# Leaky slope in PSUM instead of weight-product passes, for the second part of batch 0's MLP blocks

## The chip, the cores and the metric

The kernel runs on one core of one Trainium2 chip. The metric is device time in microseconds (us), the median of the runs.

## The reference

The program is a long convolution by FFT, gated, followed by a two-layer MLP with a leaky ReLU. Cut to what matters:

```python
def _attn_ref(x, v, pos_emb, w1, w2):                 # x, v: (2, 12480, 128)
    h_filt = (np.maximum(pos_emb @ w1, 0.0) @ w2) * window
    u = x * v
    y = irfft(rfft(u, 2*S) * rfft(h_filt, 2*S))[:, :S]   # per batch and channel
    return x * y

def _moe_ref(x, w_in, w_out):                         # 24960 tokens, 128 -> 2048 -> 128
    h = x @ w_in
    g = np.maximum(0.01 * h, h)
    return g @ w_out
```

## The kernel before, in words

The convolution is done as a two-level transform. After an opening stage that transforms batch 0, the MLP starts and runs over `NTL` = 50 blocks of tokens, `widths` columns each: block 0 has 390, the others 512 except block 24 (314) and blocks 48 and 49 (352). Blocks 0 to 24 are batch 0, blocks 25 to 49 batch 1. Each block is worked in `NF` = 16 steps, one for each 128 rows of the hidden layer. Step number `i = k * NF + f` is the clock of everything else: the main loop at the end of `tile_conv_mlp` calls, for each step, `m1(k, f)`, then `m2` of the step `DEEP` = 3 earlier, then the work that `steps` has put down for that step (loads, the inverse transforms `front` of later tokens, the sums `join`), then parts of `finish` for the block before, and lastly pieces of `conv`, the generator that carries batch 1's forward and inverse transforms. All pieces of `conv` are spread evenly over the steps before `SLOTS` (375, that is block 23, step 7). Instructions of an engine run in the order in which this loop issues them.

`m1` makes one tile `mh` of the hidden layer: three TensorE passes of 512 columns (the product is split in high and low parts, `w_in_h` times `zh` and `zl`, `w_in_l` times `zh`) into a PSUM bank, then the non-linearity, and from it the two parts `rh` and `rl`, which `m2` multiplies by `w_out_h` and `w_out_l` in three further passes into the accumulator bank `acc0` or `acc1` (`acc{k % 2}`). There are three ways to the non-linearity:

- `sums(k)`: ScalarE takes the plain ReLU from PSUM as `rh`, VectorE takes max(h, 0) - rh as `rl`; the missing slope, 0.01 times h, comes from three more passes of the block's input `zh`, `zl` by the product of the two weight matrices (`wc_h`, `wc_l`), which `m2` issues at its step 0.
- `wide`: ScalarE writes the leaky ReLU (`Lrelu`, slope 0.01) back into the same PSUM bank; `rh` is copied from there by VectorE where f is odd and by ScalarE where f is even; VectorE takes `rl` from the bank as the difference.
- else (the blocks `OWN`, 2 to 4): the leaky ReLU goes to a buffer in SBUF, and the two parts are taken from there.

`sums(k)` holds for blocks 0, 1 and 5 to 23. In batch 0, tokens that don't go by `sums` are first multiplied by 1/0.99 in `product_of` (`nc.scalar.mul` on `zf`), since the output weights are held times 0.99.

PSUM has eight banks: `mh` three, `cv` two (for `conv`, until it has ended; then for every fourth and fifth `mh` tile of the wide blocks), `io` one, `acc0` and `acc1`. In block k the bank `acc{(k + 1) % 2}` holds the sums of block k - 1 until `finish` has copied them (step 2), and the next block's from step 3 of that block on; `last_transform` uses it for the second of a pair of inverse transforms (`second`; the first of the pair is in `leads`; both are worked at step `turn_at`).

A tile of the `mh` ring can be written again once `rl` of the tile that had the bank is made; and `m2` of step i - 3, right behind `m1` of step i on TensorE, reads that same `rh` and `rl`.

Of the kernel before, what the change touches and what calls it, by code (L numbers as in the profile page):

```python
# [8 lines left out]
F32 = mybir.dt.float32  # L9
# [15 lines left out]
WIDE = 512  # L25
# [5 lines left out]
def tile_conv_mlp(ctx, tc, x, v, pos_emb, w1, w2, w_in, w_out, cf, cr, cg, cb, ci, cw, out):  # L31
    nc = tc.nc
    B, S, D = x.shape
    FO = pos_emb.shape[1]
    DFF = w_in.shape[1]
    NF = DFF // 128
# [72 lines left out]
    def mixed(t):  # L109

        return t.rearrange("p (h i) -> p i h", h=2)

    def plain(t):

        return t.rearrange("p (i h) -> p h i", h=2)

    def split2(t):

        return t.rearrange("p (h i) -> p h i", h=2)
# [44 lines left out]
    def back(dp, parts, c):  # L164

        for s in range(2):
            for j, w in halves(c):
                m = mixed if even(w) else lambda t: t
                three(dp[s][:, w], (mi_h[j][:, s], mi_l[j][:, s]), (m(parts[0][:, s, w]), m(parts[1][:, s, w])))

    def turned(pool, psum, m2, m1):

        ph = pool.tile([128, 2, KH + 1], F32, tag="ph0", name="ph0", bufs=1)
# [62 lines left out]
    with tc.manual_schedule():  # L236
# [228 lines left out]
        def conv1b():  # L465
# [46 lines left out]
            for c in range(NCH + 1):  # L512
# [5 lines left out]
                if c < NCH:  # L518
                    n = chunk(c)[1]
                    w = n * D  # L520
                    h, (th, tl) = hd.pop(c), parts.pop(c)
                    yield
                    up = psc["next"]()
                    for s in range(2):
                        three(up[s][:, :w], (mb_h[:, s], mb_l[:, s]),
                              [i[:, :n, s, :].rearrange("p (h k) d -> p k d h", h=2) for i in (th, tl)])
                    yield

                    us, p1 = sc.tile([128, 2048], F32, tag="s4", name="usp").rearrange(
                        "a (i s w) -> i a s w", i=2, s=2)  # L530
                    ph = pool.tile([128, 2, 512], F32R, tag="ph", name="ph", bufs=1)
                    pl = pool.tile([128, 2, 512], F32R, tag="pl", name="pl", bufs=1)
                    pins[c] = ph, pl
                    for s in range(2):
                        nc.scalar.mul(split2(us[L, s, :w]), plain(up[s][H, :w]), -1.0)
                        o = 1 - s
                        nc.vector.tensor_tensor(out=split2(p1[:, o, :w]), in0=plain(up[o][:, :w]),
                                                in1=split2(h[:, 0, o, :w]), op=ALU.mult)
                        if s:
                            sums(us, p1, h, 0, w)  # L540
                        yield
                        nc.scalar.copy(split2(us[H, s, :w]), plain(up[s][L, :w]))
                        yield
                    sums(us, p1, h, 1, w)
# [41 lines left out]
        ld, cin, z, acc = {}, {}, {}, {}  # L586
# [103 lines left out]
        with ExitStack() as st:  # L690
# [73 lines left out]
            def two(tag):  # L764
                return [psb.tile([128, 512], F32, tag=tag, name=tag + "p", bufs=2) for _ in range(2)]
# [41 lines left out]
            for i, c in enumerate(ORD):  # L807
# [17 lines left out]
                t, es = bins.pop(c), eh.pop(c)  # L825
                hp = two("h")
# [47 lines left out]
        ps = ctx.enter_context(tc.tile_pool(name="ps", bufs=1, space=bass.MemoryType.PSUM, reuse_waits="tile"))  # L874
# [11 lines left out]
        at0 = [sum(widths[:i]) for i in range(len(widths) + 1)]  # L886
        NTL = len(widths)
        assert at0[-1] == total * TOK

        OWN = (2, 3, 4)  # L890
        LAST = NTL // 2 - 1

        def sums(k):
            return at0[k] < S and k not in OWN and k < LAST

        def pieces_of(t):

# [34 lines left out]
        def product_of(t, zt):  # L932

            zp = ps.tile([128, 4, 128], F32, tag="io", name="zp")
            for q in range(4):
                nc.tensor.transpose(zp[:, q, :GAP], zt[:GAP, q, :], ident[:GAP, :GAP])  # L936
            zf = sm.tile([128, TOK], F32, tag="zf", name="zf", bufs=1)
            for w in range(2):
                nc.scalar.copy(zf[:, :2 * NA - 2].rearrange("d (m a) -> d m a", m=2)[:, :, w::2],
                               zp[:, 2:4, 64 * w:64 * w + KH - w])  # L940
            nc.scalar.copy(zf[:, 2 * NA - 2:].rearrange("d (m i w) -> d m w i", m=2, w=2),
                           zp[:, 0:2].rearrange("d m (w i) -> d m w i", w=2)[:, :, :, :KH])
            for k, a, c, n in pieces_of(t):
                if k not in z:
                    z[k] = [sm.tile([128, WIDE], F32R, tag=g, name=g, bufs=ZB) for g in ("zh", "zl")]
                zh, zl = (i[:, a:a + n] for i in z[k])
                if at0[k] < S and not sums(k):
                    nc.scalar.mul(zf[:, c:c + n], zf[:, c:c + n], 1 / 0.99)
                nc.scalar.copy(zh, zf[:, c:c + n])  # L949
                (nc.gpsimd if t else nc.vector).tensor_tensor(out=zl, in0=zf[:, c:c + n], in1=zh, op=ALU.subtract)  # L950
            yield
# [32 lines left out]
        def m1(k, f):  # L984
            w = widths[k]
            zh, zl = (mixed(i[:, :w]) for i in z[k])
            wide = not sums(k) and k * NF >= SLOTS
            spare = wide and (k * NF + f) % 5 > 2
            hp = ps.tile([128, WIDE], F32, tag="cv" if spare else "mh", name="mh", bufs=2 if spare else 3)[:, :w]
            fs = slice(f * 128, f * 128 + 128)  # L990
            for i, (u, m) in enumerate(((w_in_h, zh), (w_in_l, zh), (w_in_h, zl)) if k == f == 0 else
                                       ((w_in_h, zh), (w_in_h, zl), (w_in_l, zh))):
                nc.tensor.matmul(hp, u[:, fs], m, start=(i == 0), stop=(i == 2))  # L993
            rh = sm.tile([128, WIDE], F32R, tag="rh", name="rh", bufs=DEEP + 2)[:, :w]
            rl = sm.tile([128, WIDE], F32R, tag="rl", name="rl", bufs=DEEP + 2)[:, :w]
            if sums(k):
                nc.scalar.activation(out=split2(rh), in_=plain(hp), func=AF.Relu)  # L997
                nc.vector.scalar_tensor_tensor(out=split2(rl), in0=plain(hp), scalar=0.0, in1=split2(rh),  # L998
                                               op0=ALU.max, op1=ALU.subtract)
            elif wide:  # L1000
                nc.scalar.activation(out=hp, in_=hp, func=AF.Lrelu, alpha=0.01)  # L1001
                if f % 2:
                    nc.vector.tensor_copy(split2(rh), plain(hp))  # L1003
                else:
                    nc.scalar.copy(split2(rh), plain(hp))  # L1005
                nc.vector.tensor_tensor(out=split2(rl), in0=plain(hp), in1=split2(rh), op=ALU.subtract)  # L1006
            else:
                tag, pool, bufs = ((("th", psc["pool"], 1), ("tl", psc["pool"], 1), ("ct1", psc["pool"], 1),
                                    ("ph", psc["pool"], 1), ("pl", psc["pool"], 1)) if k in OWN else
                                   (("s1", s0, 3), ("hd", psc["pool"], 2), ("ct1", psc["pool"], 1),  # L1010
                                    ("s1", s0, 3), ("hd", psc["pool"], 2)))[f % 5]
                r = pool.tile([128, 2048 if tag == "hd" else 1024], F32R if tag in ("th", "tl", "ph", "pl") else F32,
                              tag=tag, name="r", bufs=bufs)[:, :w].bitcast(F32)
                nc.scalar.activation(out=split2(r), in_=plain(hp), func=AF.Lrelu, alpha=0.01)
                if f % 2:
                    nc.vector.tensor_copy(rh, r)
                else:
                    nc.scalar.copy(rh, r)
                nc.vector.tensor_tensor(out=rl, in0=r, in1=rh, op=ALU.subtract)
            return rh, rl  # L1020
# [76 lines left out]
        leads = {t - 1 for t in second}  # L1097
        turn_at = {total: NTL * NF}
# [85 lines left out]
        SLOTS = ends[NT] - 14  # L1184
# [29 lines left out]
        for k in range(NTL):  # L1214
            for f in range(NF):
                i = k * NF + f
                pend.append((k, f, m1(k, f)))
                if len(pend) > DEEP:
                    m2(*pend.pop(0))
                for s_ in steps.get(i, ()):  # L1220
                    do(*s_, i)
                if f == DEEP - 1 and k:
                    fin = finish(k - 1)
                if f >= DEEP - 1 and (f - DEEP + 1) % 2 == 0:
                    next(fin, None)
                if i < SLOTS:
                    while done < min(pieces, pace(i)):
                        next(conv, None)
                        done += 1
# [71 lines left out]
```

## Time and profile before

| what | value |
|---|---|
| time, median of 3 runs | 1609.13 us (lowest 1602.2) |
| the profiled execution | 1607.94 us, span on the core 1606.1 us |
| TensorE busy | 1552.2 us, 97% of the span |
| VectorE busy | 1137.9 us, 71% |
| ScalarE busy | 997.1 us, 62% |
| GpSimd busy | 766.7 us, 48% |
| granted TensorE clock, mean | 0.985 |

All times of the trace are counted from the first instruction. Busy time of an engine is the union of its instructions' spans; PE is TensorE's matmuls, PEld its weight loads, DVE is VectorE, ACT ScalarE, POOL GpSimd, SP the queue that issues most transfers. The matmuls overlap, so a pass takes less of TensorE's time than its own duration says. A line number is that of the kernel before.

### The profile page before, as it was taken

Reading aid. Unit: us, or ns where it says so; the run is one execution under the profiler, and the core shown is the slowest. Engines: PE = TensorE matmul, PEld = TensorE weight load, DVE = VectorE, ACT = ScalarE, POOL = GpSimd, SP = SyncE. Lnnn points to the kernel's source line nnn. Section 1 sums busy time; section 2 is a strip of 40 time slices with the busy share of each in tenths; the row PEclk is TensorE's granted clock in tenths of the full one; section 3 lists DMA queues with packets and bytes.
Section 4 is the critical chain, followed back from the end, with each engine's and each line's share of the span. In section 5 each row is a group of like instructions: output and inputs, shape, how many; then the busy total and the mean of one; then the engine's idle time right before and its main releaser. Section 6 shows DMA issues by size and latency. Waiting matters only on the chain.

```text
span 1606.1 us, 27353 instructions
## 1 busy us (share of the span) xinstructions
PE 1552.2 (97%) x9173; PEld 1318.8 (82%) x9173; DVE 1137.9 (71%) x1785; ACT 997.1 (62%) x2108; POOL 766.7 (48%) x806
## 2 busy tenths in 40 slices
PE   7995999899999999999999999999999999999998
PEld 7884555588888888888888888988888888888888
DVE  6884888656985565666676775677777777777776
ACT  2331544446655476777776766667777676777776
POOL 6772212145754275867777774543443433334310
PEclk9997999999999999999999999999999999999999
DMA  9997999866767466756656661421212212121200
GB/s 273 305 314 250 318 317 335 256 196 189 227 199 220 132 190 185 206 158 182 173 167 180 172 163 37 130 86 58 73 54 64 79 58 90 52 64 61 64 11 21
DMA packets 166268, 253.30 MB, mean 158 GB/s; under 512 B 14240, under 2 KB 118932, under 8 KB 163056
## 3 DMA queue, kind: packets, MB, share of 16 engines
q1 hardware_dynamic: 146388, 226.28, 47.4%
q10 hardware_dynamic: 19740, 25.28, 4.6%
q8 instruction: 73, 1.20, 0.3%
q14 instruction: 67, 0.55, 0.1%
HBM read 168.03 MB, written 83.43 MB: 157 GB/s over the span
## 4 chain that ended last, share of the span: by engine, by line
PE 75%; DMA 12%; DVE 7%; ACT 2%; issue 2%; SPq 1%; POOL 0%; ACTq 0%; DVEq 0%; POOLq 0%
PE mh L993 28%; PE acc L1035 9%; PE acc L1034 9%; PE acc L1036 9%; PE yp L917 4%; PE cv L143 3%; DMA scr<-o 3%; PE cv L438 3%; DMA scr<-ct 3%; PE op L1066 2%; PE a L392 2%; PE up L129 2%; PE zp L936 1%; DMA ft<-in_cf_dram 1%; PE dp L157 1%
## 5 line engine op out<-in xcount | busy, mean ns | idle before, releaser
L998 DVE SCALAR_TENSOR_TENSOR rl<-mh,rh 128x512 fp32r<-128x512 f32 (+1 forms) x336 | 226.9, 682 | 203.2 <-ACT rh L997 201.8
L1006 DVE TENSOR_TENSOR rl<-mh,rh 128x512 fp32r<-128x512 f32 (+2 forms) x416 | 277.1, 670 | 83.7 <-ACT rh L1005 75.1
L1001 ACT ACTIVATE mh<-mh 128x512 f32<-128x512 f32 (+2 forms) x416 | 236.4, 569 | 154.1 <-PE mh L993 141.1
L993 PE MATMUL mh<-zh,w_in_h 128*128 128x512 f32 (+3 forms) x800 | 316.8, 396 | 3.4 <-DVE rl L998 2.3
L993 PE MATMUL mh<-zl,w_in_h 128*128 128x512 f32 (+3 forms) x800 | 300.1, 375 | 0.0
L993 PE MATMUL mh<-zh,w_in_l 128*128 128x512 f32 (+3 forms) x800 | 299.9, 375 | 0.0
L1035 PE MATMUL acc<-rl,w_out_h 128*128 128x512 f32 (+3 forms) x800 | 299.3, 374 | 0.1
L1034 PE MATMUL acc<-rh,w_out_h 128*128 128x512 f32 (+3 forms) x800 | 299.3, 374 | 0.0
L1036 PE MATMUL acc<-rh,w_out_l 128*128 128x512 f32 (+3 forms) x800 | 299.0, 374 | 0.0
L997 ACT ACTIVATE rh<-mh 128x512 fp32r<-128x512 f32 (+1 forms) x336 | 198.9, 595 | 138.8 <-PE mh L993 130.1
L950 POOL TENSOR_TENSOR zl<-zf,zh 128x390 fp32r<-128x390 f32 (+24 forms) x110 | 68.4, 634 | 402.4 <-ACT zh L949 386.1
L680 POOL TENSOR_TENSOR cp<-cq,cp 98x256 f32<-98x256 f32 x248 | 193.3, 780 | 31.4 <-DVE cp L668 14.7
L1003 DVE CAST rh<-mh 128x512 fp32r<-128x512 f32 (+2 forms) x208 | 139.3, 670 | 65.9 <-ACT mh L1001 65.6
L993 PEld LDWEIGHTS mh<-zh,w_in_h 128*128 128x128 f32 x800 | 151.9, 190 | 29.4 <-DVE rl L998 8.4
L993 PEld LDWEIGHTS mh<-zh,w_in_l 128*128 128x128 f32 x800 | 151.9, 190 | 19.8
L1035 PEld LDWEIGHTS acc<-rl,w_out_h 128*128 128x128 f32 x800 | 151.3, 189 | 20.3 <-DVE rl L1006 0.4
L1034 PEld LDWEIGHTS acc<-rh,w_out_h 128*128 128x128 f32 x800 | 151.3, 189 | 19.8
L1036 PEld LDWEIGHTS acc<-rh,w_out_l 128*128 128x128 f32 x800 | 151.3, 189 | 19.8
L993 PEld LDWEIGHTS mh<-zl,w_in_h 128*128 128x128 f32 x800 | 152.3, 190 | 15.2 <-DVE zl L982 0.2
L1005 ACT CAST rh<-mh 128x512 fp32r<-128x512 f32 (+2 forms) x208 | 118.5, 570 | 6.5
L677 POOL TENSOR_TENSOR cq<-cin 98x256 f32<-98x256 f32 x124 | 97.1, 783 | 0.5 <-DMA cin<-scr 0.4
L138 POOL TENSOR_TENSOR pin<-ta,tb 128x512 f32<-128x512 f32 (+1 forms) x23 | 28.8, 1252 | 134.9 <-DVE tb L137 134.9
(166 smaller groups left out, 2545.7 us busy)
## 6 DMA issues: line engine op xcount, KB each, us to landing
cin<-scr SPq DMA_DIRECT2D x318, 98.0 KB
hd<-hspec SPq DMA_DIRECT2D x48, 512.0 KB
bin<-scr SPq DMA_DIRECT2D x24, 768.0 KB
scr<-o SPq DMA_DIRECT2D x28, 588.0 KB
scr<-ct SPq DMA_DIRECT2D x25, 512.0 KB
scr1b<-o SPq DMA_DIRECT2D x32, 392.0 KB
hspec<-hs ACTq DMA_DIRECT2D x48, 256.0 KB
xm<-in_x_dram SPq DMA_DIRECT2D x128, 96.0 KB
```

The source lines that it names most:

```text
L677: eng.tensor_tensor(out=cq[:, p], in0=ci_t[:, 0, :, 0, :], in1=ci_t[:, 0, :, 1, :], op=op)
L680: eng.tensor_tensor(out=cp[:, p, w], in0=cq[:, p], in1=cp[:, p, 1], op=op)
L993: nc.tensor.matmul(hp, u[:, fs], m, start=(i == 0), stop=(i == 2))
L997: nc.scalar.activation(out=split2(rh), in_=plain(hp), func=AF.Relu)
L998: nc.vector.scalar_tensor_tensor(out=split2(rl), in0=plain(hp), scalar=0.0, in1=split2(rh), op0=ALU.max, op1=ALU.subtract)
L1001: nc.scalar.activation(out=hp, in_=hp, func=AF.Lrelu, alpha=0.01)
L1003: nc.vector.tensor_copy(split2(rh), plain(hp))
L1005: nc.scalar.copy(split2(rh), plain(hp))
L1006: nc.vector.tensor_tensor(out=split2(rl), in0=plain(hp), in1=split2(rh), op=ALU.subtract)
L1034: nc.tensor.matmul(ap, w_out_h[:, f, :], rh, start=(f == 0 and not sums(k)), stop=False)
L1035: nc.tensor.matmul(ap, w_out_h[:, f, :], rl, start=False, stop=False)
L1036: nc.tensor.matmul(ap, w_out_l[:, f, :], rh, start=False, stop=(f == NF - 1))
```

## The change

`sums` now ends at block 8 instead of block 24: the sixteen blocks 8 to 23 are `wide`. They lose the three weight-product passes at the start of `m2`, their tokens are multiplied by 1/0.99, and their non-linearity is made in place in PSUM by `Lrelu`, with a copy and a difference behind it. Before `SLOTS` three steps of a block (6, 10 and 14, unless a pair of transforms is due within two steps) take the idle accumulator bank for `mh` in place of one of the three; from `SLOTS` on, two steps of five take a `cv` bank.

```diff
         OWN = (2, 3, 4)
-        LAST = NTL // 2 - 1
+        LEAK = 8
 
         def sums(k):
-            return at0[k] < S and k not in OWN and k < LAST
+            return at0[k] < S and k not in OWN and k < LEAK
 
@@ in m1 @@
             zh, zl = (mixed(i[:, :w]) for i in z[k])
-            wide = not sums(k) and k * NF >= SLOTS
-            spare = wide and (k * NF + f) % 5 > 2
-            hp = ps.tile([128, WIDE], F32, tag="cv" if spare else "mh", name="mh", bufs=2 if spare else 3)[:, :w]
+            i = k * NF + f
+            wide = not sums(k) and k >= LEAK
+            tag, bufs = "mh", 3
+            if i >= SLOTS:
+                tag, bufs = ("cv", 2) if i % 5 > 2 else ("mh", 3)
+            elif wide and f in (6, 10, 14) and not any(-2 <= i - turn_at[t] <= 2 for t in leads):
+                tag, bufs = f"acc{(k + 1) % 2}", 1
+            hp = ps.tile([128, WIDE], F32, tag=tag, name="mh", bufs=bufs)[:, :w]
```

## Rows read from the trace of the kernel before

**Rows 1.** The page's part 1: busy us (share of the span) and instructions per engine

```profile
PE 1552.2 (97%) x9173; PEld 1318.8 (82%) x9173; DVE 1137.9 (71%) x1785; ACT 997.1 (62%) x2108; POOL 766.7 (48%) x806
```

**Rows 2.** Busy time by windows: stretch, length, each engine's busy us, clock, DMA share

```profile
564.40:997.10 432.70, 427.84 (x2272) 368.27 (x2271) 288.54 (x397) 314.07 (x657) 307.19 (x298) 1.00 0.60 167
1059.80:1499.30 439.50, 439.50 (x2406) 382.55 (x2405) 325.80 (x481) 314.62 (x662) 170.13 (x246) 1.00 0.21 66
```

**Rows 3.** The same windows view for line 993 alone: PE and PEld busy

```profile
564.40:997.10 432.70, 200.07 (x720) 132.19 (x720) 1.00 0.60 167
```

**Rows 4.** Waits from 564.4 to 1018.9 us: total us, times, longest us

```profile
PEld mh L993 <- DVE rl L998: 8.2, 16, 1.1
PE cv L143 <- ACT ct L223: 2.0, 1, 2.0
ACT rh L997 <- PE mh L993: 93.5, 109, 4.0
ACT ct L223 <- DMA scr<-ct: 9.7, 3, 6.3
```

**Rows 5.** Timeline, TensorE in batch 0: start us, length us, line, out<-in; consecutive tiles' first passes

```profile
640.67 0.38 PE L993 MATMUL mh<-zh,w_in_h 128*128 128x512 f32 x1
641.96 0.38 PE L993 MATMUL mh<-zh,w_in_h 128*128 128x512 f32 x1
```

**Rows 6.** Groups of instructions, TensorE, 564.4 to 1018.9 us: count | busy us, mean ns

```profile
L1030 PE MATMUL acc<-zh,wc_h 128*128 128x512 f32 x16 | 6.1, 379 | 0.0
```

**Rows 7.** Groups, ScalarE: batch 0's stretch first, batch 1's (1059.8 to 1499.3 us) behind it

```profile
L997 ACT ACTIVATE rh<-mh 128x512 fp32r<-128x512 f32 x257 | 153.7, 601 | 95.9 <-PE mh L993 93.5
...
L1001 ACT ACTIVATE mh<-mh 128x512 f32<-128x512 f32 x305 | 178.5, 585 | 118.7 <-PE mh L993 107.9 <-DVE rh L1003 1.4
L1005 ACT CAST rh<-mh 128x512 fp32r<-128x512 f32 x152 | 89.1, 586 | 4.7
```

**Rows 8.** Single lines: ns min/median/max; L948 whole run, L949 564.4 to 997.1 us

```profile
L948 ACT ACTIVATE zf<-zf x8: 218/427/536, 346.7 to 992.9; 128x268 f32<-128x268 f32 x1, 128x244 f32<-128x244 f32 x1, 128x146 f32<-128x146 f32 x1, 128x366 f32<-128x366 f32 x1
...
L949 ACT CAST zh<-zf x35: 199/397/522, 584.0 to 993.4; 128x390 fp32r<-128x390 f32 x5, 128x318 fp32r<-128x318 f32 x1, 128x72 fp32r<-128x72 f32 x1, 128x50 fp32r<-128x50 f32 x1
```

**Rows 9.** Groups, VectorE: batch 0's stretch (two rows), then batch 1's

```profile
L998 DVE SCALAR_TENSOR_TENSOR rl<-mh,rh 128x512 fp32r<-128x512 f32 x256 | 174.2, 688 | 146.9 <-ACT rh L997 146.2
...
L668 DVE TENSOR_TENSOR cp<-cin 98x256 f32<-98x256 f32 x36 | 32.5, 915 | 0.0
...
L1006 DVE TENSOR_TENSOR rl<-mh,rh 128x512 fp32r<-128x512 f32 x305 | 209.6, 691 | 62.6 <-ACT rh L1005 56.2
L1003 DVE CAST rh<-mh 128x512 fp32r<-128x512 f32 x152 | 105.1, 691 | 51.1 <-ACT mh L1001 51.1
```

**Rows 10.** Timeline, a tile of batch 0: its third pass and its rl

```profile
641.10 0.38 PE L993 MATMUL mh<-zh,w_in_l 128*128 128x512 f32 x1
...
642.15 0.69 DVE L998 SCALAR_TENSOR_TENSOR rl<-mh,rh 128x512 fp32r<-128x512 f32 x1 [0.42 <-ACT rh L997]
```

**Rows 11.** Timeline, a tile of batch 1: third pass, and rl (the second of two merged)

```profile
1086.85 0.38 PE L993 MATMUL mh<-zh,w_in_l 128*128 128x512 f32 x1
...
1087.87 1.32 DVE L1006 TENSOR_TENSOR rl<-mh,rh 128x512 fp32r<-128x512 f32 x2
```

**Rows 12.** Busy time by windows: blocks 2 and 3, then blocks 5 and 6

```profile
379.50:443.80 64.30, 64.08 (x420) 56.76 (x420) 56.80 (x71) 41.87 (x84) 46.06 (x40) 1.00 0.72 215
473.50:538.60 65.10, 65.10 (x431) 58.42 (x430) 38.02 (x61) 30.70 (x65) 27.52 (x27) 1.00 0.73 212
```

**Rows 13.** Timeline, end of block 14: VectorE's sums for a transform, and a late tile

```profile
767.78 2.85 DVE L668 TENSOR_TENSOR cp<-cin 98x256 f32<-98x256 f32 x2
...
771.88 0.48 PE L993 MATMUL mh<-zh,w_in_h 128*128 128x512 f32 x1 [0.49 <-DVE rl L998]
```

**Rows 14.** Busy time by windows around the longest gap of TensorE in the stretch

```profile
634.20:637.10 2.90, 0.94 (x5) 0.73 (x5) 0.00 (x0) 1.45 (x4) 0.00 (x0) 0.99 0.68 265
637.10:640.50 3.40, 3.40 (x10) 2.63 (x9) 2.41 (x5) 3.29 (x8) 1.72 (x2) 0.50 0.21 59
```

## The prediction

> **What bounds the kernel now.** I read the page first: TensorE is busy 97% of a span of 1606.1 us [rows 1]. Such an average says nothing of a stage, so I went on to the windows. The blocks that change are 8 to 23. Blocks 8 to 22 are the stretch from 564.4 to 997.1 us: line 993 stands there with 720 passes, 15 blocks of 16 tiles of three passes [rows 3]. TensorE is busy in 427.8 of its 432.7 us, so it waits 4.9 us in all; ScalarE is busy 314.1 us (73%), VectorE 288.5 us (67%) [rows 2]. So TensorE's queue sets the time of this stretch, and the others have room. The waits view says what the 4.9 us are: weight loads of `mh` waiting for a late `rl` (16 times), and one wait for `ct`; ScalarE, for its part, mostly waits for TensorE (93.5 us) [rows 4]. The reader should see a stage bound by TensorE, in which ScalarE's and VectorE's answers come back just in time with a few exceptions.
>
> **What is removed.** Three weight-product passes in each of 16 blocks, 48 in all, of which line 1030 is one third [rows 6]. Their own duration, 379 ns, is not what they cost: passes overlap. The first passes of two neighbouring tiles lie 1.29 us apart with six passes of the same size between them [rows 5], so a pass takes 0.215 us of the queue. 48 x 0.215 = 10.3 us, on the engine that sets the time. That is all that can be had: 0.64% of the run, 0.645 us in each block. (Even with the 4.9 us of waits gone too, the gain would be 15.2 us.)
>
> **What is added on ScalarE.** The in-place leaky ReLU costs 585 ns where the plain one costs 601, and where f is even a copy of 586 ns is added [rows 7]. For the 240 tiles of blocks 8 to 22: -240 x 0.016 + 120 x 0.586 = +66.5 us. The product with 1/0.99 has a median of 427 ns; it runs once for each piece of which `zh` is cast, and there are 35 such casts in the stretch [rows 8]: +15 us, somewhat less since block 24's have it already. ScalarE goes from 314.1 to about 394 us.
>
> **What is added on VectorE.** The difference costs 691 ns against 688, and 120 copies of 691 ns come in [rows 9]: +84 us, from 288.5 to about 372 us. GpSimd, SP and the DMA queues get nothing new; no transfer is moved.
>
> Without the passes, TensorE needs 427.8 - 15 x 0.645 = 418.1 us. So ScalarE would be at 94% and VectorE at 89% of that. All three sums are below the time of TensorE, so it keeps the stage if the queues stay in step. What decides is whether they do.
>
> **What gets later.** A tile's bank and its `rl` are wanted three steps on. Today, with nothing in its way, `rl` is done 1.36 us after the tile's third pass (642.84 less 641.48) [rows 10]; by the way of batch 1 it is 1.96 us (1089.19 less 1087.23) [rows 11]. So each tile comes back 0.60 us later, before any queueing. In a run of steps with no convolution pass between them, the third pass of one tile and the first of the third tile after it lie 3 x 1.29 - 0.65 = 3.2 us apart: of 1.9 us to spare 1.25 are left. Queued behind a late `Lrelu` on ScalarE are its copy, the evacuation of `cv` (whose bank the next convolution pass waits for) and the copies of the fronts; behind a late `rl` on VectorE, the next tile's copy.
>
> The bursts are where this ends in a stall. VectorE's pair of sums for a tile of transforms takes 2 x 0.915 us, 18 such pairs in the stretch [rows 9]; at the end of block 14 one took 2.85 us, and TensorE then waited 0.49 us for `rl` [rows 13]. ScalarE's burst at a front gets up to two products longer.
>
> The accumulator bank works against this: with three tiles of sixteen out of the ring, those of steps 7 to 15 get their bank a whole step (1.29 us) later than it came free. But `m2` of the tile three steps back still stands right behind `m1`, so only the three passes between, 0.65 us, are won for `rl`.
>
> **The price of the new stalls, bounded.** Below: nothing, if the bank gives back what the chain took. Nearest row: blocks 2 and 3 already go by `Lrelu`, blocks 5 and 6 by the sums, and each pair has four transforms and the same even share of the convolution. The first pair takes 64.3 us, the second 65.1 [rows 12]: 0.8 us won where the passes alone give 1.29, so 0.25 us a block is lost, 4 us over 16 blocks. VectorE there is at 88% (56.8 of 64.3), as it would be here; but ScalarE is at only 65% (41.9), and the leaky ReLU frees the PSUM bank at once. Here ScalarE is at 94%, so I go above that row. Above: each of some 21 transforms (16 x 512 columns, 390 in each) costs the 0.60 us, a copy of 0.586 and two products of 0.427, or 2.0 us each: 42 us. Between: the 16 places where `rl` is late today [rows 4] each get the 0.60 us and about 0.5 us of longer queue (half of each burst meets a copy more): 17.6 us, of which the freed bank covers about half. I take 9 us, nearer to the row than to the upper end, since the sums of all engines still fit.
>
> **The sum.** -10.3 + 9 = -1.3 us against the profiled execution of 1607.9 us: 1606.6, say 1607 us. That execution lies 1.2 us below the median of the runs shown (1609.1), whose lowest is 1602.2.
>
> **The rivals.**
>
> *The gain arrives whole.* New stalls stay under 3 us: the bank and the slow steps (those with convolution passes between) take up the lag. For it: batch 1's stretch runs the same tiles with TensorE busy in all of its 439.5 us [rows 2]. Against it: there ScalarE is at 72% and VectorE at 74%, and five banks serve the ring. Time: 1607.9 - 10.3 + 0 to 3 = 1598 to 1601 us.
>
> *ScalarE becomes the bound (slower).* At 94% the queue of ScalarE runs behind in each block with no transforms, where TensorE's steps are shortest, and TensorE stalls at the ring's bank. For it: the 94%, and ScalarE's own waits of up to 6.3 us for the store of `ct` [rows 4], in which everything behind stands. Against it: it now spends 93.5 us waiting for TensorE, which it would not if it were behind. It decides from 0.645 us of stalls a block. At 1.5 to 2.5 us a block, 24 to 40 us less 10.3: 1622 to 1638 us.
>
> The Trainium skill (Perfetto Trace Analysis, section Identifying the Most-Contended Engine) speaks for this rival: it takes ScalarE's occupancy as a fair measure, but judges TensorE by the busy share of its weight loads and not of its matmuls. By that rule TensorE is at 85% here (368.3 of 432.7) and ScalarE at 94% after the change would be the bound, 1622 us or more. Batch 1's row weighs against reading 85% as room: weight loads are busy 87% there (382.6 of 439.5) in a stretch in which TensorE never waits [rows 2]. So the rule gets this rival's chance and no more.
>
> *The clock falls with the stalls.* After a gap of 1.96 us in TensorE's work (2.90 less 0.94) the granted clock was 0.50, the lower of its two levels (1.2 GHz), for 3.4 us [rows 14]; at half speed that costs 1.7 us more. The shorter gaps of the stretch show no such fall. If the new stalls came as about ten gaps of 2 us, each with its slow stretch, that is 10 x 3.7 - 10.3 = +27 us: 1635 us. Against it: only one gap of that size stands here now, and it hangs on a store, which the change doesn't touch.
>
> **How the numbers follow.** Gain mostly eaten, stalls of 4 to 14 us (1602 to 1612): 0.55. Gain whole (1598 to 1601): 0.20. ScalarE the bound (1612 to 1638): 0.20. The clock: 0.05. The predicted time is that of the likeliest, 1607 us. The range of eight in ten takes in the gain whole and the nearer half of ScalarE's case: 1598 to 1624 us. Two per cent, about what a measurement of this kernel can tell from no change, is 32 us. Faster by that is out of reach of a gain of 15.2 us at most: 0.01, for a run unlike those shown. Slower by that needs 2.65 us of stalls a block, the far end of ScalarE's case or the clock's: 0.06. Within: 0.93.
>
> **What would show it.** Lines 1030 to 1032 should have 48 fewer records in all (63 to 15), line 1001 some 672 in place of 416, line 948 some 40 in place of 8. From block 8 to block 22 ScalarE should be busy about 394 us and VectorE about 372, TensorE's matmuls 10 us less; the waits view should show more than 16 waits of `mh` for `rl` (now line 1006), some 14 us in place of 8.2. Blocks 24 to 49 should take what they take now. I am wrong in the size of the stalls if TensorE's idle time in the stretch is under 8 or over 20 us; wrong in the mechanism if it waits for `cv` or for a transform's `zh` and not for `rl`, or if the clock falls more than once.

## The result, and the profile after

The changed kernel takes 1623.1 us (median; 1621.9 to 1625.0) against 1608.4 us for the kernel before: a ratio of 1.0107, 95% interval 1.0093 to 1.0122. It is slower, by some 17 us going by the ratio, where a gain of 1.3 us was forecast. One of the six runs of the kernel before took 3284 us and is left out of the ratio, though not of its median. The time lies inside the stated range, at its very end.

The windows view of the changed kernel (stretch, length, busy us and count of PE, PEld, DVE, ACT, POOL, then clock, DMA share, GB/s) for blocks 8 to 22, from block 8's first pass to block 23's, and for all from block 24 on:

```profile
563.00:1012.30 449.30, 427.86 (x2228) 359.38 (x2227) 356.93 (x517) 385.77 (x812) 306.74 (x298) 0.99 0.58 161
...
1033.40:1620.60 587.20, 583.05 (x3286) 511.81 (x3285) 433.40 (x660) 417.57 (x899) 212.30 (x306) 1.00 0.20 63
```

The stretch that took 432.7 us [rows 2] takes 449.3: 16.6 us more, which is the whole difference (the two profiled executions differ by 14.5 us in all, since what lies ahead of block 8 and block 23 were 2.1 us shorter this time). Everything behind block 24 takes 587.2 us; in the kernel before, too, it takes 587.2. TensorE is idle for 21.4 us of the stretch (449.3 less 427.9) where it was for 4.9.

In all profiled executions of this study, what lies behind block 24 takes 587.1 to 587.3 us, while what lies ahead of block 8 takes 559 to 569 us, which doesn't go by the edits. So below the whole run is compared by the ratio, and causes by the length of blocks 8 to 22 alone, found in each trace from the same two passes.

The waits view of the changed kernel from 563.0 to 1012.3 us, TensorE and its weight loads (total us, times, longest us), to be read beside [rows 4]:

```profile
PE mh L998 <- DVE rl L1011: 15.5, 13, 3.4
PE acc L1039 <- DVE rh L1008: 1.6, 3, 1.2
PE acc L1040 <- DVE rl L1011: 1.5, 6, 0.3
...
PEld acc L1040 <- DVE rl L1011: 5.7, 14, 0.7
PEld mh L998 <- ACT mh L1006: 4.9, 7, 1.2
PEld mh L998 <- DVE rl L1011: 4.2, 5, 1.6
```

The kernel before, for TensorE itself, from 564.4 to 1018.9 us:

```profile
PE mh L993 <- DVE rl L998: 2.3, 4, 0.7
PE cv L143 <- ACT ct L223: 2.0, 1, 2.0
```

(The lines of `m1` behind its first few, and all of `m2`, stand five further down than before: 998 was 993, 1006 was 1001, 1008 was 1003, 1011 was 1006, 1039 was 1034.) TensorE's wait for a PSUM bank whose `rl` isn't made yet has become the main one: 15.5 us where it was 2.3, up to 3.4 us at a time. The groups view of the same stretch shows the added work at the durations that [rows 7, 9] gave:

```profile
L1006 ACT ACTIVATE mh<-mh 128x512 f32<-128x512 f32 x240 | 140.0, 588 | 43.0 <-PE mh L998 37.0 <-DVE rh L1008 3.9 <-DVE tl L496 0.7
L1010 ACT CAST rh<-mh 128x512 fp32r<-128x512 f32 x120 | 70.3, 586 | 3.8
...
L1008 DVE CAST rh<-mh 128x512 fp32r<-128x512 f32 x120 | 82.4, 687 | 48.5 <-ACT mh L1006 48.0
```

The timeline of the changed kernel at its longest wait (start us, length us) shows how one comes about:

```profile
592.61 0.59 ACT L1006 ACTIVATE mh<-mh 128x512 f32<-128x512 f32 x1
593.35 2.85 DVE L668 TENSOR_TENSOR cp<-cin 98x256 f32<-98x256 f32 x2
594.50 0.38 PE L1041 MATMUL acc<-rh,w_out_l 128*128 128x512 f32 x1
596.13 0.68 DVE L496 TENSOR_TENSOR tl<-bin,th 128x512 fp32r<-128x512 f32 x1
596.73 0.68 DVE L1008 CAST rh<-mh 128x512 fp32r<-128x512 f32 x1
597.44 1.29 DVE L1011 TENSOR_TENSOR rl<-mh,rh 128x512 fp32r<-128x512 f32 x2
598.28 0.76 PE L998 MATMUL mh<-zh,w_in_h 128*128 128x512 f32 x1 [3.40 <-DVE rl L1011]
```

The `Lrelu` of block 8's last tile, an odd one, is done at 593.20. Its copy is VectorE's, and stands behind two sums for a transform and a difference for the convolution, until 596.73. Only then come its `rl` and that of the next tile, both kept waiting; TensorE, which wants the first tile's bank, stands still from 594.88 to 598.28. Before, ScalarE alone made `rh`, and one VectorE operation for each tile, not two, stood behind such a pair. At this place the kernel before stood still for 0.69 us ([rows 13] shows the like at the end of block 14):

```profile
596.60 0.48 PE L993 MATMUL mh<-zh,w_in_h 128*128 128x512 f32 x1 [0.69 <-DVE rl L998]
```

In the changed kernel a stretch at the lower clock level (1.2 GHz) begins within the gap, here 6.8 us long:

```profile
597.20:604.00 6.80, 5.72 (x14) 4.57 (x15) 4.34 (x8) 2.97 (x7) 5.05 (x7) 0.50 0.84 222
```

Over all 240 tiles of the stretch, the time from the end of a tile's third pass to the end of its `rl` was 2.21 us on average before and is 3.65 us now. 40 tiles took longer than the 3.2 us that the prediction allows in a run of short steps; now 140 do. (By the ends that the trace gives to passes, the third pass ends 0.81 us after the first starts, and the room is 3 x 1.29 - 0.81 = 3.06 us: 44 tiles before, 155 now.) Station by station, a tile now waits 1.17 us on average until ScalarE takes it up (0.54 before), and 1.20 us from the end of ScalarE's first operation to the start of `rl` (0.38 before), in which the copy is made. The first operation (0.6 us) and `rl` (0.69) take what they took.

### The profile page after: what moved, and what is told of

It is laid out like the page before. It is cut to its first block, busy times and chain, and to the rows that moved or that the text cites. A ratio compares the mean times of both kernels' runs of the same rounds, so it can differ in the third digit from the quotient of the medians.

```text
span 1620.6 us, 27650 instructions
## 1 busy us (share of the span) xinstructions
PE 1550.2 (96%) x9125; PEld 1309.2 (81%) x9125; DVE 1214.9 (75%) x1913; ACT 1073.0 (66%) x2273; POOL 762.9 (47%) x806
## 4 chain that ended last, share of the span: by engine, by line
PE 71%; DMA 9%; DVE 8%; ACT 6%; issue 3%; SPq 1%; POOL 1%; ACTq 0%; DVEq 0%; POOLq 0%
PE mh L998 27%; PE acc L1040 9%; PE acc L1041 9%; PE acc L1039 9%; PE yp L917 4%; PE cv L438 3%; PE cv L143 3%; DMA scr<-ct 2%; ACT mh L1006 2%; PE up L129 2%; PE op L1071 1%; PE a L392 1%; DMA scr<-o 1%; PE dp L157 1%; PE zp L936 1%
## 5 line engine op out<-in xcount | busy, mean ns | idle before, releaser
L1011 DVE TENSOR_TENSOR rl<-mh,rh 128x512 fp32r<-128x512 f32 (+2 forms) x672 | 451.8, 677 | 125.9 <-ACT rh L1010 111.2
L1006 ACT ACTIVATE mh<-mh 128x512 f32<-128x512 f32 (+2 forms) x672 | 385.7, 576 | 203.2 <-PE mh L998 183.0
L998 PE MATMUL mh<-zh,w_in_h 128*128 128x512 f32 (+3 forms) x800 | 317.8, 397 | 16.5 <-DVE rl L1011 15.5
L1008 DVE CAST rh<-mh 128x512 fp32r<-128x512 f32 (+2 forms) x336 | 227.3, 677 | 115.4 <-ACT mh L1006 114.5
L1010 ACT CAST rh<-mh 128x512 fp32r<-128x512 f32 (+2 forms) x336 | 193.3, 575 | 10.6
L1039 PEld LDWEIGHTS acc<-rh,w_out_h 128*128 128x128 f32 x800 | 151.6, 190 | 23.3 <-DVE rh L1008 3.2
L1003 DVE SCALAR_TENSOR_TENSOR rl<-mh,rh 128x512 fp32r<-128x512 f32 (+1 forms) x80 | 52.6, 664 | 56.4 <-ACT rh L1002 55.8
L560 POOL TENSOR_TENSOR pl<-usp,ph 128x512 fp32r<-128x512 f32 (+1 forms) x50 | 63.7, 1283 | 51.5 <-ACT ph L559 51.3
```

What stands on the lines that cost most here:

```text
L1039: nc.tensor.matmul(ap, w_out_h[:, f, :], rh, start=(f == 0 and not sums(k)), stop=False)
```

## Theories

The 10.3 us of the removed passes should be there, so some 27 us have been added. A and B were written down at once, C only when e1 to e4 had been measured:

- **A, VectorE's bursts**: the pairs of sums of line 668, with a copy now queued behind them. 14.4 of the 21.4 us of idle time stand within a few us behind one.
- **B, ScalarE's load**: ScalarE binds the stage (the slower rival of the prediction).
- **C, the ring**: no engine is full; each tile's return through both queues is longer, three banks with a loan don't cover it, and lateness of either queue is paid alike.

## The experiments

All are told in this table. The third column is the time in which no pass of TensorE runs there, the fourth the length of the stretches at the lower clock; columns two to four are from one profiled execution each. The ratio is to runs of the kernel before made beside each run, whose medians were 1605.7 to 1608.4 us.

| run | blocks 8 to 22, us | TensorE idle, us | lower clock, us | median, us | ratio to before (95% interval) |
|---|---|---|---|---|---|
| before | 432.7 | 4.9 | 3.4 | 1608.4 | 1 |
| after | 449.3 | 21.4 | 10.2 | 1623.1 | 1.0107 (1.0093 to 1.0122) |
| e1_sums_pool | 440.4 | 16.9 | 0 | 1618.0 | 1.0059 (1.0036 to 1.0082) |
| e2_before_sums_pool | 430.3 | 4.6 | 0 | 1605.0 | 0.9987 (0.9975 to 0.9999) |
| e3_sums_apart | 442.2 | 16.7 | 3.4 | 1618.9 | 1.0071 (1.0051 to 1.0092) |
| e4_no_products | 443.8 | 19.2 | 6.8 | 1619.6 | 1.0073 (1.0047 to 1.0099) |
| e5_before_no_passes | 422.6 | 5.6 | 0 | 1595.5 | 0.9940 (0.9921 to 0.9959) |
| e6_no_acc_bank | 454.5 | 26.6 | 6.8 | 1629.9 | 1.0158 (1.0130 to 1.0186) |
| e7_four_of_sixteen | 447.3 | 23.3 | 0 | 1624.2 | 1.0121 (1.0098 to 1.0143) |
| e8_pool_folded | 434.2 | 13.4 | 0 | 1610.5 | 1.0033 (1.0018 to 1.0048) |
| e9_more_on_dve | 434.4 | 12.5 | 3.4 | 1606.3 | 1.0004 (0.9986 to 1.0022) |
| e11_only_dve_copies | 435.7 | 14.7 | 0 | 1608.4 | 1.0016 (1.0002 to 1.0031) |
| e12_only_act_copies | 435.0 | 12.3 | 6.8 | 1607.3 | 1.0001 (0.9988 to 1.0014) |
| e13_one_slope_pass | 425.8 | 5.7 | 3.4 | 1595.1 | 0.9931 (0.9904 to 0.9958) |

How far this stretch varies between executions of one kernel was not measured. One wait for the store of `ct` ([rows 4]; 1.4 to 2.7 us) stands in some of these executions and not in others, in some of them with 3.4 us at the lower clock behind it (before, e9, e13), and no edit is aimed at it. So a difference of less than some 4 us in the second column shows nothing by itself.

### e5_before_no_passes: the first term alone

```diff
-            if f == 0 and sums(k):
+            if f == 0 and sums(k) and k < 8:
                 ... the three weight-product passes ...
-            nc.tensor.matmul(ap, w_out_h[:, f, :], rh, start=(f == 0 and not sums(k)), stop=False)
+            nc.tensor.matmul(ap, w_out_h[:, f, :], rh, start=(f == 0 and not (sums(k) and k < 8)), stop=False)
```

> The kernel before without the weight-product passes in blocks 8 to 23 and with nothing in their place: it leaves the slope of 0.01 out of those blocks. It measures the first term of the sum alone. If a pass costs its 0.215 us of TensorE's queue: blocks 8 to 22 take 9.7 us less than the 432.7 us of before, the run 10.3 us less (1597 us). Rival: the passes are cover, time in which late tiles come back, and without them TensorE waits instead: 2 to 5 us less.

Measured: 422.6 us, 10.1 us less than before (9.7 expected; before has 1.7 us of lower clock that e5 hasn't), and 0.60% off the whole run. The windows view of this run's blocks 8 to 22:

```profile
562.70:985.30 422.60, 416.97 (x2227) 358.42 (x2227) 288.18 (x397) 313.39 (x657) 307.32 (x298) 1.00 0.60 171
```

The passes were no cover: TensorE is idle 5.6 us without them, 4.9 with them. So the price of the leaky way is 449.3 - 422.6 = 26.7 us, three times what the sum allowed (9 us).

### e1_sums_pool and its control e2_before_sums_pool: VectorE's bursts

```diff
-            eng = nc.vector if t == 0 or 8 <= t < NT else nc.gpsimd
+            eng = nc.vector if t == 0 else nc.gpsimd
```

> The changed kernel (1623 us) with one thing moved: for the transforms 8 to 31 the two sums at the head of a join (line 668, 36 in the stretch, 2.6 to 3.1 us a pair when they run one behind the other) go to GpSimd instead of VectorE. Theory A, VectorE's bursts: TensorE's idle time behind these pairs (14.4 of the 21.4 us in blocks 8 to 22) goes, and with it the stretches at the lower clock: 1603 to 1609 us, unless GpSimd's own chain gets late. Theory B, ScalarE's load: ScalarE has the same work, so the time stays within 3 us of 1623 us.

> The kernel before with the same move (line 668 to GpSimd for transforms 8 to 31), as the control of the run above: what the move is worth without the change. Theory A: little is to be had, since only about 2 us of TensorE's 4.9 us of idle time stand behind such a pair: 1604 to 1609 us; GpSimd, at 71% of the stretch, gets some 27 us more (36 x 0.75), and if its chain then comes late for the convolution's passes, it is slower by up to 10 us. Theory B says the same.

Measured: 8.9 us less than the changed kernel in the stretch (440.4), where A wanted 14 or more and B next to nothing. In the kernel before the same move gains 2.4 us, of which 1.7 us are lower clock that stands in before and not here. By the median, too, e1 (1618.0 us) lies between A (1603 to 1609) and B (within 3 us of 1623). So the bursts are part of it, and no more. The waits view of e1 from 569.0 to 1009.4 us shows what came in their place:

```profile
PE mh L998 <- DVE rl L1011: 6.2, 8, 2.2
PE acc L1040 <- DVE rl L1011: 2.5, 8, 0.8
PE mh L998 <- ACT ct L223: 1.8, 1, 1.8
PE mh L998 <- ACT ph L559: 1.3, 1, 1.3
```

With the pairs gone, tiles were still late, less so and in other places.

### e3_sums_apart: the same work, the pair split

```diff
-            yield from join_hi(t)
-            yield from join_lo(t)
+            hi, lo = join_hi(t), join_lo(t)
+            if not 8 <= t < NT:
+                yield from hi
+                yield from lo
+                return
+            for g, n in ((hi, 1), (lo, 3), (hi, 1), (lo, 3)):
+                for _ in range(n):
+                    next(g)
+                    yield
```

> The changed kernel with the two VectorE sums of a join set apart: the first one, GpSimd's three operations for the first half, the second one, GpSimd's other three. Each engine has exactly the work it had; only the pair is no longer one block in VectorE's queue. Theory A: at half the length a burst leaves two of three tiles in time; a half to two thirds of the 14.4 us go: 1611 to 1617 us. Theory B: no change, 1621 to 1625 us.

Measured: 442.2 us, 7.1 less, with no engine's work changed; 4.7 us of it are idle time, most of the rest lower clock. The median, 1618.9 us, lies between A (1611 to 1617) and B (1621 to 1625): the order in VectorE's queue alone is worth more than B allows, and less than A.

### e4_no_products: ScalarE's load

```diff
-                if at0[k] < S and not sums(k):
+                if at0[k] < S and not sums(k) and not LEAK <= k < NTL // 2 - 1:
                     nc.scalar.mul(zf[:, c:c + n], zf[:, c:c + n], 1 / 0.99)
```

> The changed kernel without the products by 1/0.99 for the tokens of blocks 8 to 23 (line 948, some 35 of 0.43 us in ScalarE's queue, 15 us); it leaves that factor out of the result. Theory A: the fronts' copies come a little earlier, 1620 to 1624 us. Theory B, ScalarE's load: 15 us of work less on the engine that binds, 1608 to 1614 us.

Measured: 443.8 us, 5.5 less, for 12.7 us less in ScalarE's queue (373.1 against 385.8 us busy). It lies between A (up to 3) and B (9 to 15); the median, 1619.6 us, is at A's edge. Neither theory stands alone after these four.

### e6_no_acc_bank and e7_four_of_sixteen: the ring

```diff
-            elif wide and f in (6, 10, 14) and ...
+            elif False and wide and f in (6, 10, 14) and ...      # e6
+            elif wide and f in (4, 8, 12, 15) and ...             # e7
```

> The changed kernel without the loan of the accumulator bank before SLOTS: all mh tiles of blocks 8 to 22 on the three banks. No engine gets more or less work. Theory C, the ring: a tile now holds its bank 0.6 us and a queue's lag longer, and three banks are too few for it; without the loan it gets clearly worse, 8 us or more over the 449.3 us that blocks 8 to 22 take in the changed kernel. Theories A and B alone (VectorE's bursts, ScalarE's load): the engines set the pace, within 3 us of it.

> The changed kernel with the loan on steps 4, 8, 12 and 15 instead of 6, 10 and 14: one tile of sixteen more out of the ring, and the loan begins earlier in the block. Theory C, the ring: blocks 8 to 22 take 3 to 6 us less than 449.3. Theories A and B alone: within 2 us of it.

Measured: without the loan 454.5 us, 5.2 more, and the whole run is slower too (1.0158 against 1.0107, the intervals apart). That is the way of C, on the same work, but less than the 8 us that C expected. The waits view of e6 from 562.0 to 1016.5 us shows the loan's effect where it acts, in waits for a bank (24 against 13 in the changed kernel):

```profile
PE mh L998 <- DVE rl L1011: 22.7, 24, 3.0
```

With the fourth tile the stretch takes 447.3 us, 2.0 less, and the whole run no less. C expected 3 to 6, and the 2.0 don't speak for it: TensorE is idle for 1.9 us more than in the changed kernel, and the stretch is shorter only because the clock didn't fall. The waits view of e7 from 569.1 to 1016.3 us:

```profile
PE mh L998 <- DVE rl L1011: 11.5, 12, 2.6
PE acc L1039 <- DVE rh L1008: 4.8, 5, 1.5
PE mh L998 <- ACT ot L1058: 2.4, 3, 1.4
```

TensorE waits less for a bank of the ring (11.5 us against 15.5), and more for `rh` in `m2` (4.8 against 1.6) and for the accumulator bank, which `finish` is still copying when step 4 wants it.

### e8_pool_folded: both relieved

```diff
+            whole = all(at0[p[0]] < S and not sums(p[0]) for p in pieces_of(t))
+            take = (lambda o, i: nc.scalar.mul(o, i, 1 / 0.99)) if whole else nc.scalar.copy
             for w in range(2):
-                nc.scalar.copy(zf[...], zp[...])
+                take(zf[...], zp[...])
             ... the same for the third copy; the product of line 948 only where not whole ...
```

and the edit of e1.

> The changed kernel with VectorE's sums on GpSimd (as in e1) and with the product by 1/0.99 made in the copies that take zp out of PSUM, which run anyway, where a transform's tokens all need it (so line 948 goes, as in e4, and the result keeps the factor). e1 took 8.9 us and e4 5.5 us off the 449.3 us of blocks 8 to 22. If VectorE's and ScalarE's lateness add up in one chain, both together take off 14 us: 435 us, within 3 us of the 432.7 of before; if either hides the other, less than 11 us.

Measured: 434.2 us, 15.1 less than the changed kernel, where the two alone gave 8.9 and 5.5, or 14.4 together. They add up, as far as single executions tell: lateness of VectorE's and of ScalarE's queue is paid one on top of the other.

### e11_only_dve_copies, e12_only_act_copies: half the leaky way each

```diff
-            if sums(k):
+            if sums(k) or LEAK <= k < NTL // 2 - 1 and f % 2 == 0:    # e11; e12: f % 2 == 1
                 nc.scalar.activation(out=split2(rh), in_=plain(hp), func=AF.Relu)
```

> The changed kernel with the leaky way only for the odd tiles of blocks 8 to 23, whose copy VectorE makes; the even tiles take the plain ReLU as before (the slope is left out there). VectorE has the load of the changed kernel, ScalarE is relieved of its 120 copies (70 us). Blocks 8 to 22 take 422.6 us without the passes and 449.3 with the whole leaky way: 26.7 us to share out. Theory A, VectorE's queue: 442 us or more. Theory B, ScalarE's load: 430 or less. Theory C, the ring and both queues in one chain: about half, 434 to 438 us.

> The mirror of the run above: the leaky way only for the even tiles, whose copy ScalarE makes; the odd tiles take the plain ReLU (the slope is left out there). ScalarE has the load of the changed kernel, VectorE is relieved of its 120 copies (83 us). Theory A: 430 us or less for blocks 8 to 22. Theory B: 442 or more. Theory C: 434 to 438 us.

The windows view of blocks 8 to 22, e11:

```profile
565.40:1001.10 435.70, 421.00 (x2227) 356.85 (x2226) 360.99 (x517) 324.39 (x691) 306.68 (x298) 1.00 0.60 166
```

and e12:

```profile
565.30:1000.30 435.00, 422.72 (x2228) 360.08 (x2227) 280.42 (x398) 386.31 (x812) 307.17 (x298) 0.99 0.60 166
```

Measured: 435.7 and 435.0 us, that is 13.1 and 12.4 over the 422.6 of e5, together 25.5 of the 26.7. e11 has VectorE as full as the changed kernel and ScalarE 61 us emptier; e12 the reverse, by 77 us. Each costs about half. The halves are not quite clean: both runs carry all the products by 1/0.99 (45 records of line 948 in each, as in the changed kernel) and the loan, and e12 has 6.8 us at the lower clock where e11 has none. But A and B are both ruled out as the whole cause, and C's forecast (434 to 438) holds in both.

### e9_more_on_dve: the balance

```diff
-                if f % 2:
+                if f % 2 or f % 8 == 4 and at0[k] < S:
                     nc.vector.tensor_copy(split2(rh), plain(hp))
```

on top of e8.

> e8 (the changed kernel with VectorE's sums on GpSimd and the folded product, 434.2 us for blocks 8 to 22) with the copies of batch 0 shared five to three instead of four to four: 30 more on VectorE (+21 us, to about 360), 30 fewer on ScalarE (-18 us, to about 355). Theory B, ScalarE is what still binds: 428 to 431 us. Theory A: 437 us or more. Theory C: within 2 us of 434.2, since what one queue wins the other loses.

Measured: 434.4 us against 434.2. 15 us went from ScalarE's queue (372.7 to 357.4 us busy) to VectorE's (340.3 to 355.4). The mean return of a tile stayed as well (3.36 us, 3.35 in e8): the wait until ScalarE takes a tile up fell by 0.13 us, the way from there to `rl` grew by as much, as C expected. This is weaker than it looks, though. e9's stretch has a wait of 1.9 us for the store of `ct` and 3.4 us of lower clock, and e8's has neither (its wait is 0.4 us); without them some 3 us would have been won, and by the ratios, too, e9 lies 0.3% below e8. B's forecast (428 to 431) is not excluded by this run alone.

### e13_one_slope_pass: a version faster than both

```diff
                 nc.tensor.matmul(ap, wc_h, zh, start=True, stop=False)
-                nc.tensor.matmul(ap, wc_h, zl, start=False, stop=False)
-                nc.tensor.matmul(ap, wc_l, zh, start=False, stop=False)
```

on the kernel before, with the edit of e1.

> A version that tries to get the gain of the passes without the longer chain: the kernel before with VectorE's sums on GpSimd (e2) and one weight-product pass in place of three; it leaves the two passes with the low parts of the input and of the weight product out of the slope term. If a pass costs 0.215 us and is no cover, 42 passes less in 21 blocks give 9.0 us, of them 6.5 in blocks 8 to 22 (430.3 to 423.8 us): 1594 to 1598 us, 0.7% under the kernel before.

The windows view of its blocks 8 to 22:

```profile
559.30:985.10 425.80, 420.15 (x2242) 362.64 (x2241) 266.58 (x361) 313.24 (x657) 329.23 (x335) 1.00 0.61 170
```

Measured: a ratio of 0.9931 (0.9904 to 0.9958), 1595.1 us: faster than the kernel before and the changed one. The run lies in the range expected (1594 to 1598). The stretch takes 4.5 us less than e2's, not 6.5; in it one wait of a convolution pass for ScalarE's copy of `ct`, 2.7 us long, stands ahead of a stretch of 3.4 us at the lower clock, where e2 waits 1.6 us and its clock doesn't fall. Two thirds of the passes were to be had by leaving them out, with the tiles no later (a mean return of 2.16 us, 2.12 in e2). The slope term is less exact for it; what that does to the output isn't shown here.

## Why the prediction was wrong

**What bounds the kernel: right.** TensorE's queue sets the pace; blocks 24 to 49 are unchanged, and the counts of lines 1030 to 1032 (15), 1001 (672) and 948 (45) came about as forecast. One reading was wrong: the 4.9 us of idle time are not the 16 late weight loads, which sum to 8.2 us and overlap running passes. TensorE itself waited for a late `rl` at 4 places, 2.3 us, and 2.0 us for `ct`.

**What is removed: right.** 0.215 us a pass, 9.7 us for 15 blocks; e5 measured 10.1, with 1.7 us of clock in it.

**What is added: right in kind, somewhat high.** ScalarE is busy 385.8 us (394 forecast), VectorE 356.9 (372), with the durations of [rows 7, 9]; the subtractions of line 496 alone took 10 us less than before (992 ns on average, 1204 before). As shares of what the stretch now takes, that is 86% and 79%.

**What gets later: the step that failed.** The 0.60 us by which a tile's return grows was read from [rows 10, 11], two tiles whose queues were all but empty. The average return grew by 1.44 us. The other 0.84 us are queueing, most of it in front of ScalarE (0.63 us more until it takes a tile up). The prediction put queueing at 0.5 us, and only at the 16 places where a weight load waited for `rl` already [rows 4]. The tiles that came over the limit had not been just under it: 0.60 us more for each tile of the kernel before would have put 56 of the 240 over 3.2 us, the measured mean of 1.44 us would have put 138, and 140 were.

**The price of the new stalls: 9 us in the sum, 26.7 measured.** The nearest row, blocks 2 and 3 against 5 and 6 [rows 12], misled: 0.25 us a block there, 26.7 / 15 = 1.8 here. VectorE was as full there; what differed is that the leaky value went to SBUF, so that the bank was free after one operation, and that ScalarE was at 65%. Both were named in the prediction as reasons to go above the row, and given too little; no run separated the two. The upper bound of 42 us held. Of the 26.7 us (against e5), 15.8 are idle time of TensorE (21.4 less 5.6), and 4.3 the clock (in 6.8 and 3.4 us at half speed TensorE was busy for 5.7 and 2.9; none in e5). The other 6.6 us are waits that no idle time shows. The ends of the matmuls are modelled, and a late pass can start while the one before still counts as running. By the starts of the passes, 0.216 us apart where nothing holds them, such lateness sums to 25.2 us in the changed kernel and 18.9 in e5: 6.3 us more, 3.9 of it at passes of `m2`.

**The loan of the accumulator bank.** Taken as covering about half of 17.6 us; e6 measures 5.2.

**The signs.** The prediction's own signs say so too: TensorE's idle time, 21.4 us, is over the 20 that it named for the size of the stalls. The clock fell twice in the stretch, and by its words ("more than once") that counts against the mechanism; but the clock is 4.3 of the 26.7 us, and the main wait is the one it named, `mh` for `rl`.

**The rivals.** The time (1623) is that of "ScalarE becomes the bound", but its mechanism isn't what happened: e11 and e12 charge both engines about alike, and e9 takes 15 us off ScalarE and puts them on VectorE for 3 us at most. What did happen of it is that ScalarE's queue ran late and TensorE stalled at the ring's bank. The same goes for the rule of the Trainium skill (Perfetto Trace Analysis, Identifying the Most-Contended Engine): the runs don't agree that the engine with the highest occupancy, ScalarE here, is the one to relieve first. 18 us less on VectorE won 8.9 (e1), 12.7 us less on ScalarE won 5.5 (e4), about as much for each. The clock fell once more than before, so that rival is about a sixth of the price and not the cause. "The gain arrives whole" took five banks and slack queues in batch 1; neither was there.

**What stays open.** How the 26.7 us divide between tiles that hold a bank too long and tiles whose `rl` is too late for `m2`: the changed kernel's waits name the bank (15.5 us) more than `m2` (3.1 us, 7.0 with those that no idle time shows), but both come from the same late tiles, and e7 only moved waits from one to the other. No run freed a bank early with `rl` as late as now, or had a fourth bank of its own.

## What to carry to other kernels

When work is moved off a full engine onto two that are three quarters full, don't ask only whether their sums still fit: ask how long one tile's way through their queues becomes on average, against the steps that its buffers allow. The longer chain of operations is only a part of that. Here it added 0.60 us, and the fuller queues 0.84 us on top, for all tiles and not only for those already late. A price read from another stage of the same kernel may not hold where the buffer is given back at another point of the chain, or another engine is fuller. And before an operation is replaced, measure what leaving it out gives (e5): that ceiling, here 10 us, is soon eaten.

## What the runs showed of the hardware

The sums of line 668, two SBUF inputs of 98x256, vary by seven, in one form. From the view of this line in the changed kernel (ns min/median/max):

```profile
L668 DVE TENSOR_TENSOR cp<-cin x50: 409/419/2793, 315.1 to 966.5; 98x256 f32<-98x256 f32 x50
```

It goes with what GpSimd is doing: of the 26 that started with GpSimd idle, or with less than 0.1 us left of its instruction, all took 409 to 427 ns; of the 24 that started while it had more to do, 22 took 474 to 2793 (in the kernel before 30 of 31 took 408 to 427, and 19 of 19 took 494 to 2486). In the timeline above a pair of them takes 2.85 us, while in the trace GpSimd works on the convolution's products (lines 501 and 502) from 593.25 to 595.92. The Trainium skill (SBUF — State Buffer, SBUF: two separate sides) says that VectorE with two SBUF inputs and a GpSimd instruction that reads SBUF lock each other out of a shared pair of ports for a whole instruction, whichever starts first; the spread agrees with that, though no run here took GpSimd's work away to show it.

The clock doesn't fall by the length of a gap alone. After gaps of 3.40 us (594.9) and 2.98 us (775.6) the changed kernel ran at the lower level for 6.8 and 3.4 us; after one of 2.96 us (688.0) it did not (windows view; the last line is the fall behind the gap at 775.6):

```profile
688.00:691.00 3.00, 0.05 (x1) 0.08 (x1) 2.97 (x6) 1.27 (x3) 2.84 (x3) 1.00 0.97 243
...
690.90:694.30 3.40, 3.35 (x16) 2.98 (x17) 2.49 (x4) 2.39 (x7) 2.69 (x4) 1.00 0.98 252
...
778.10:781.50 3.40, 2.94 (x7) 2.43 (x8) 2.87 (x6) 1.17 (x3) 2.13 (x3) 0.50 0.97 220
```

The kernel before had fallen after 1.96 us [rows 14]; in e7, whose longest gap is 2.62 us, it did not fall in the stretch at all.
